# Three of four weight sums moved behind the third addition of a result, in a kernel of local attention and two expert layers

## The chip, the cores and the metric

One core of a Trainium2 chip runs the whole program. The metric is the device time of one execution in microseconds (us). Before the change it is 838.9 us, the median of three runs (838.24 to 839.41).

## The reference

The computation has three stages on 2 x 768 tokens of 512 channels. The change is in the third, where each token's channels go through four experts, weighted by normalized probabilities:

```python
def _moe2_ref(x, domain_probs, w1, w2):
    p = domain_probs / (domain_probs.sum(-1, keepdims=True) + 1e-09)
    out = np.zeros((N, D), dtype=np.float32)       # N = 1536, D = 512, E = 4, F = 1024
    for e in range(E):
        h = np.maximum(x @ w1[e], 0.0)
        out += p[:, e:e + 1] * (h @ w2[e])
    return out
```

Ahead of it stand attention (a window of 16 positions and block summaries) and a layer of 512 to 2048 to 512 channels with a PReLU.

## The kernel before

Every matrix operand is split in two parts of reduced precision, a high one (a copy on ScalarE) and a remainder (a subtraction on GpSimd or VectorE), and a product is three matmuls.

The third stage runs in 32 units `s`: 16 quarters of an expert (256 of the 4 x 1024 hidden channels) for each of two halves of the tokens; `NQ` = `UA` = 16. In a unit `e_steps` makes the first-layer products by a scheme of seven multiplications of quarter matrices (`p1` to `p7`), which needs sums of weight quarters (`e_sums`) besides the quarters. In the first half of the tokens (and in the last two units) `l2b` multiplies the hidden values by the second-layer weights, in six results of 128 tokens: six matmuls accumulate in a PSUM tile of pool `ps_2` (three buffers), and one VectorE instruction multiplies by the probability and adds to `acc2` (line 824; line 822 in the first unit of a half). In units 16 to 29, of the second half, the second layer uses a scheme of seven multiplications too, and that needs four sums of second-layer weights from two neighbouring units. They are made in advance, in the first half, and stored to DRAM (`dt`): `t_sums` makes them on VectorE, in place in the raw weight tiles `rb` (line 437), and `t_split` makes high part (ScalarE, line 441) and remainder (GpSimd, line 442) of each and stores both (line 416). Seven units do so, those with odd `s` from 1 to 13, each 28 / 7 = 4 subtractions of 128x512.

The order of the work. `standard(s, ...)` runs a unit: the products of the first layer, with the last two of the unit before it among them (`p1`, `p4` of the unit before, `p2`, `p6`, `p3` of the unit before, `p5`, `p7`), and then the six results `l2b` of the unit before, among which `merge` spreads the steps of `e_prep(s + 1)`: the loads, splits and sums for the next unit. In the seven units these are 14 steps: `t_sums`, the split of A11 and A12, `e_sums`, the splits of S1 and S2, of S3 and S4 and of A22, a load, two splits of second-layer weights, a load, and the four `t_split`. A split is one copy on ScalarE (line 386), one remainder on GpSimd (line 387) and stores.

TensorE and ScalarE execute in the order of the code (`tc.manual_schedule` with these two engines). The order on VectorE, GpSimd and the queue of SyncE that issues the DMAs is set by a planner when the program is built: it takes, by its own estimates, an instruction whose operands are ready, and of several ready ones the one that stands earlier in the code. `tc.issue_after(ins)` puts what is traced in its block behind `ins` on the queue of `ins`'s engine; `mark[s, 1, 1]` is the VectorE instruction that ends the result of `p7` of unit `s` (line 690).

ScalarE copies the PSUM tile `cb` of `p1` (line 678, tile `p`) before `p6` accumulates further into `cb` (line 655).

Of the kernel before, what the change touches and what calls it, by code (L numbers as in the profile page):

```python
# [12 lines left out]
ALU = mybir.AluOpType  # L13
# [79 lines left out]
def kernel(  # L93
# [15 lines left out]
    nc = tc.nc  # L109
# [22 lines left out]
    acc2 = acc.rearrange("p (t e) -> p t e", t=NT)  # L132
# [234 lines left out]
    def e_load_a(s):  # L367
        q = s % NQ
        t = wp.tile([P, 4, 2 * P], F32, tag="raw", name="ra", bufs=3)
        nc.sync.dma_start(out=t[:, 1:3].rearrange("p a c -> p (a c)"), in_=wb_in[0, 2 * q])  # L370
        nc.sync.dma_start(out=t[:, 0:4:3], in_=wb_in[0, 2 * q + 1].rearrange("p (a c) -> p a c", a=2))
        pw["a", s] = t

    def e_load_b(s):
        q = s % NQ
        if s % 2:
            t = gp.tile([P, 2, DM], F32, tag="rb", name="rb", bufs=1)
        else:
            t = wp.tile([P, 2, DM], F32, tag="raw", name="rb", bufs=3)
        nc.sync.dma_start(out=t, in_=wb_in[1, 2 * q:2 * q + 2].rearrange("i p n -> p i n"))  # L380
        pw["b", s] = t

    def e_split(pool, k, src, n=DM):
        hi = pool.tile([P, n], F32R, tag="h", name=f"w{k}h")
        lo = pool.tile([P, n], F32R, tag="l", name=f"w{k}l")
        nc.scalar.activation(hi, src, AF.Copy)  # L386
        nc.gpsimd.tensor_tensor(lo, src, hi.bitcast(F32), op=ALU.subtract)  # L387
        return hi, lo

    def e_sums(s):  # L390
        r = pw["a", s]
        s12 = wp.tile([P, 2, 2 * P], F32, tag="e", name="s12")
        s34 = wp.tile([P, 2, 2 * P], F32, tag="t", name="s34")

        def go(eng):
            eng.tensor_tensor(s12[:, 0], r[:, 0], r[:, 3], op=ALU.add)
            eng.tensor_tensor(s12[:, 1], s12[:, 0], r[:, 1], op=ALU.subtract)
            eng.tensor_tensor(s34[:, 0], r[:, 1], r[:, 0], op=ALU.subtract)
            eng.tensor_tensor(s34[:, 1], r[:, 2], s12[:, 1], op=ALU.subtract)

        if s % 2 == 0 and quad(s - 1 + NQ):
            with tc.issue_after(mark[s - 1, 0, 0]):
                go(nc.vector)
        else:
            go(nc.gpsimd)
        pw["s", s] = s12, s34

    def quad(s):
        return UA <= s < UB
# [4 lines left out]
    def put(dst, pair):  # L414
        for h, t in enumerate(pair):
            nc.sync.dma_start(out=dst[:, h], in_=t.bitcast(F32))
# [12 lines left out]
    def t_view(s, i):  # L429
        d = 2 * P * (i in (1, 2))  # L430
        return pw["b", s - i % 2][:, :, d:d + 2 * P]

    def t_sums(s):
        t1, t2, t3, t4 = (t_view(s, i) for i in range(4))
        with tc.issue_after(mark[s, 1, 1]):
            for y, p, q in ((t1, t3, t1), (t3, t2, t3), (t2, t2, t1), (t4, t4, t2)):
                nc.vector.tensor_tensor(y, p, q, op=ALU.subtract)

    def t_split(s, i):
        t, hi, lo = t_view(s, i), xh[t_place(i)], xl[t_place(i)]  # L440
        nc.scalar.activation(hi, t, AF.Copy)
        nc.gpsimd.tensor_tensor(lo, t, hi.bitcast(F32), op=ALU.subtract)
        put(dt[unit(s), i], (hi, lo))
# [16 lines left out]
    def named(s, names, hi, lo):  # L460
        for i, name in enumerate(names):
            ws[s, name] = hi[:, i * 2 * P:(i + 1) * 2 * P], lo[:, i * 2 * P:(i + 1) * 2 * P]

    def e_fetch(s):
        q = s % NQ
        for names in PARTS[1:3]:
            named(s, names, *get(wpool[0], lambda h: da[q, names[0]][:, h]))
        if not quad(s):
            for f in range(2):
                ws[s, f] = get(wpool[1], lambda h: dw[q, f][:, h])  # L470

    def e_load_again(s):
        if s >= 2 * NQ:
            return
        q = s % NQ
        if s == NQ:
            t = wp.tile([P, 3, 2 * P], F32, tag="raw", name="rc", bufs=3)
        else:
            t = gp.tile([P, 3, 2 * P], F32, tag="rb", name="rc", bufs=1)
        pw["a", s] = t  # L480
        nc.sync.dma_start(out=t[:, 0:2].rearrange("p a c -> p (a c)"), in_=wb_in[0, 2 * q])
        nc.sync.dma_start(out=t[:, 2], in_=wb_in[0, 2 * q + 1][:, 2 * P:])

    def e_prep(s):
        if s >= 2 * NQ:
            return []
        def part(names, src, pool=wpool[0]):
            pair = e_split(pool, 0, src, len(names) * 2 * P)
            named(s, names, *pair)
            if s < NQ and names in PARTS[1:3]:  # L490
                put(da[s, names[0]], pair)

        if s >= NQ:
            return [
                lambda: e_fetch(s),
                lambda: part(PARTS[0], pw["a", s][:, 0:2].rearrange("p a c -> p (a c)")),
                lambda: part(PARTS[3], pw["a", s][:, 2], wa22),
                lambda: e_load_again(s + 1),
            ]

        def second(i):
            ws[s, i] = e_split(wpool[1], 1, pw["b", s][:, i])
            n = 2 * P if s % 2 and quad(s + NQ) else DM
            put(dw[s, i][:, :, 0:n], [x[:, 0:n] for x in ws[s, i]])

        def flat(t):
            return t.rearrange("p a c -> p (a c)")

        steps = [
            lambda: part(("A11", "A12"), flat(pw["a", s][:, 1:3])),  # L510
            lambda: e_sums(s),
            lambda: part(("S1", "S2"), flat(pw["s", s][0])),
            lambda: part(("S3", "S4"), flat(pw["s", s][1])),
            lambda: part(("A22",), pw["a", s][:, 3], wa22),
        ]
        if s + 1 < NQ:
            steps.append(lambda: e_load_a(s + 1))
        for i in range(2):
            steps.append(lambda i=i: second(i))
        if s + 1 < NQ:  # L520
            steps.append(lambda: e_load_b(s + 1))
        else:
            steps.append(lambda: e_load_again(s + 1))
        if s % 2 == 0 and quad(s - 1 + NQ):
            steps.insert(0, lambda: t_sums(s - 1))
            steps += [lambda i=i: t_split(s - 1, i) for i in range(4)]
        return steps

# [4 lines left out]
    def split3(ps, terms):  # L533
        n = len(terms)
        for i, (a, c) in enumerate(terms):
            ins = nc.tensor.matmul(ps, a, c, start=(i == 0), stop=(i == n - 1))  # L536
        return ins
# [121 lines left out]
    bs, fs, mark = {}, {}, {}  # L659
# [150 lines left out]
    def l2b(s, i):  # L810
        b, q = divmod(s, NQ)
        t, half, e = b * NAC + i, i // (NAC // 2), q * NE // NQ
        tt = slice(i % (NAC // 2) * P, (i % (NAC // 2) + 1) * P)
        ps = ps_2.tile([P, DM], F32, tag="l2", name="l2")
        terms = []
        for f in range(2):
            (wh, wl), (gh, gl) = ws[s, f], gs[s, f, half]
            terms += [(gh[:, tt], wh), (gh[:, tt], wl), (gl[:, tt], wh)]
        split3(ps, terms)
        pe = prob_sb[:, t, e:e + 1]  # L820
        if q == 0:
            nc.vector.tensor_scalar(acc2[:, t], ps, pe, None, op0=ALU.mult)
        else:
            nc.vector.scalar_tensor_tensor(acc2[:, t], ps, pe, acc2[:, t], op0=ALU.mult, op1=ALU.add)  # L824
        if q == NQ - 1:
            nc.sync.dma_start(out=out[t * P:(t + 1) * P, :], in_=acc2[:, t])

# [7 lines left out]
    def l2_steps(u):  # L835
        n, c0, size = units[u]
        return [lambda d=d: l2a(n, d, c0, size) for d in range(KD)]
# [96 lines left out]
    with tc.manual_schedule(engines={mybir.EngineType.PE, mybir.EngineType.Activation}):  # L934
        left, keep = [], []
        l2 = l2_steps(len(units) - 1)[KD // 2:]
# [46 lines left out]
        for s in range(UA):  # L983
            l2, left, _ = standard(s, l2, left)
# [3 lines left out]
        for a in range(UA, UB, 2):  # L988
            q = l2_quad(a)
# [16 lines left out]
            old, done = q, k  # L1006
        paired(UB, "1..2..6...5..7...4...3...", old[done:], splits, 3)
        l2, left = [lambda i=i: l2b(UB, i) for i in range(NAC)], []
        for s in range(UB + 1, 2 * NQ):
            l2, left, keep = standard(s, l2, left)  # L1010
# [62 lines left out]
```

## Time and profile before

| | |
|---|---|
| median of the runs | 838.9 us (838.24 to 839.41) |
| the profiled execution, its own time | 837.95 us |
| its span, first to last instruction | 836.2 us |
| TensorE matmul busy | 814.4 us, 97% |
| TensorE weight load busy | 745.3 us, 89% |
| VectorE busy | 618.2 us, 74% |
| ScalarE busy | 427.4 us, 51% |
| GpSimd busy | 294.0 us, 35% |
| chain that ended last, TensorE's share | 92% |

Times in the trace are counted from the start of the span. PE is the matmuls of TensorE, PEld its weight loads, DVE is VectorE, ACT ScalarE, POOL GpSimd, SPq the queue of SyncE. The seven units with `t_sums` lie from 340 to 570 us, one in about 31.2 us, and repeat one another closely; the first of them is read below, where the additions are still line 822.

### The profile page before, as it was taken

The numbers are of one execution on the slowest core, as the hardware profiler recorded it, in microseconds if no ns is written. First come the engines' busy times: TensorE is split into PE (matmuls) and PEld (weight loads), VectorE is DVE, ScalarE is ACT, GpSimd is POOL, SyncE is SP. The second block draws the span as 40 slices with busy tenths as digits, with TensorE's granted clock in tenths as the row PEclk, the third lists the DMA queues.
The fourth block names the chain that finished last, engine by engine and source line by source line (L and its number), as shares of the span: only waits on it lengthen the run. The fifth ranks groups of instructions, "written<-read, shape, count | busy, mean of one in ns | idle before, by whom it ended". The sixth has DMA issues, their size and how long they took to land.

```text
span 836.2 us, 14453 instructions
## 1 busy us (share of the span) xinstructions
PE 814.4 (97%) x5000; PEld 745.3 (89%) x5000; DVE 618.2 (74%) x1315; ACT 427.4 (51%) x1050; POOL 294.0 (35%) x265
## 2 busy tenths in 40 slices
PE   3799999999999999999999999999999999999998
PEld 3699999888888888988988988988999999999997
DVE  6998667999994446587687687687667677768765
ACT  4999995543442323454454454455455454455430
POOL 0000000000013100376886886889243444354330
PEclk9799999999999999999999999999999999999999
DMA  9999412233222100266866867879776756767621
GB/s 321 283 299 298 156 46 102 101 100 102 84 92 74 53 1 0 101 223 229 304 234 231 290 215 252 289 240 321 241 228 203 256 197 229 238 217 231 200 74 75
DMA packets 97496, 155.37 MB, mean 186 GB/s; under 512 B 9872, under 2 KB 48272, under 8 KB 97424
## 3 DMA queue, kind: packets, MB, share of 16 engines
q1 hardware_dynamic: 96848, 154.18, 55.0%
q8 instruction: 39, 0.64, 0.3%
q14 instruction: 33, 0.27, 0.1%
q10 hardware_dynamic: 576, 0.28, 0.1%
HBM read 106.71 MB, written 47.71 MB: 185 GB/s over the span
## 4 chain that ended last, share of the span: by engine, by line
PE 92%; ACT 4%; DVE 2%; DMA 1%; issue 0%; ACTq 0%
PE l L536 48%; PE cb L655 16%; PE l2q L777 13%; PE cd L655 8%; PE ca L655 4%; PE s L215 1%; ACT sm L234 1%; ACT sm L253 1%; PE xps L277 1%; PE pt L259 1%; DMA alpha_sb<-in_alpha 1%; ACT ptb L152 1%; DMA kw<-in_kw 1%; DVE vs L179 0%; DVE sm L225 0%; DVE vcat L192 0%
## 5 line engine op out<-in xcount | busy, mean ns | idle before, releaser
L387 POOL TENSOR_TENSOR w0l<-ra,w0h 128x256 fp32r<-128x256 f32 (+1 forms) x32 | 36.8, 1151 | 357.4 <-ACT w0h L386 357.4
L824 DVE SCALAR_TENSOR_TENSOR acc<-l,prob_sb,acc 128x512 f32<-128x512 f32 x101 | 74.5, 745 | 24.7 <-PE l L536 24.6
L788 DVE SCALAR_TENSOR_TENSOR acc<-l2q,prob_sb,acc 128x256 f32<-128x256 f32 x156 | 71.2, 479 | 27.3 <-PE l2q L777 25.4
L536 PE MATMUL l<-xh,w0h 128*128 128x512 f32 (+1 forms) x240 | 84.6, 352 | 0.1
L536 PE MATMUL l<-gh,w1h 128*128 128x512 f32 (+1 forms) x240 | 83.4, 350 | 0.0
L536 PE MATMUL l<-xl,w0h 128*128 128x512 f32 (+1 forms) x240 | 83.3, 347 | 0.0
L536 PE MATMUL l<-xh,w0l 128*128 128x512 f32 (+1 forms) x240 | 83.2, 347 | 0.0
L536 PE MATMUL l<-gh,w1l 128*128 128x512 f32 (+1 forms) x240 | 83.0, 347 | 0.0
L536 PE MATMUL l<-gl,w1h 128*128 128x512 f32 (+1 forms) x240 | 81.5, 347 | 0.0
L536 PE MATMUL l<-w1h,gh 128*128 128x512 f32 x192 | 75.6, 394 | 0.0
L536 PE MATMUL l<-w1h,gl 128*128 128x512 f32 x192 | 75.2, 392 | 0.0
L536 PE MATMUL l<-w1l,gh 128*128 128x512 f32 x192 | 75.1, 391 | 0.0
L678 ACT ACTIVATE u<-cb 128x384 f32<-128x384 f32 x64 | 31.3, 489 | 51.7 <-PE cb L655 51.7
L561 DVE SCALAR_TENSOR_TENSOR l<-m,beta,l 128x512 f32<-128x512 f32 (+1 forms) x60 | 38.6, 646 | 23.8 <-ACT m L555 23.6
L555 ACT ACTIVATE m<-l 128x512 f32<-128x512 f32 (+1 forms) x60 | 30.6, 512 | 46.6 <-PE l L536 46.3
L536 PEld LDWEIGHTS l<-xh,w0h 128*128 128x128 f32 x240 | 45.5, 189 | 6.2 <-ACT ptb L152 0.3
L536 PEld LDWEIGHTS l<-gh,w1h 128*128 128x128 f32 x240 | 45.5, 189 | 5.7
L536 PEld LDWEIGHTS l<-gh,w1l 128*128 128x128 f32 x240 | 45.5, 189 | 5.6
L536 PEld LDWEIGHTS l<-xl,w0h 128*128 128x128 f32 x240 | 45.4, 189 | 5.5
L536 PEld LDWEIGHTS l<-gl,w1h 128*128 128x128 f32 x240 | 45.4, 189 | 5.5
L536 PEld LDWEIGHTS l<-xh,w0l 128*128 128x128 f32 x240 | 45.4, 189 | 5.6
L387 POOL TENSOR_TENSOR w0l<-s,w0h 128x512 fp32r<-128x512 f32 x32 | 47.8, 1513 | 2.9 <-ACT w0h L386 2.9
(165 smaller groups left out, 2527.7 us busy)
## 6 DMA issues: line engine op xcount, KB each, us to landing
raw<-in_wa SPq DMA_DIRECT2D x32, 512.0 KB, 3.8
rb<-in_wb SPq DMA_DIRECT2D x16, 512.0 KB, 4.5
ra<-in_wb SPq DMA_DIRECT2D x32, 256.0 KB, 3.6
dt<-xh SPq DMA_DIRECT2D x28, 256.0 KB, 3.4
dt<-xl SPq DMA_DIRECT2D x28, 256.0 KB, 4.3
bh<-dt SPq DMA_DIRECT2D x28, 256.0 KB, 3.7
bl<-dt SPq DMA_DIRECT2D x28, 256.0 KB, 3.6
q<-in_qh SPq DMA_DIRECT2D x24, 256.0 KB, 5.2
```

The costliest lines, as they stand in the source:

```text
L152: nc.scalar.activation(dst, src, AF.Copy)
L215: nc.tensor.matmul(sp[:, u], q[:, u // 2, u % 2], kw[:, :, u // 2, u % 2], start=True, stop=True)
L234: nc.scalar.activation(sm[:, u], sm[:, u], AF.Exp, bias=mx[:, u:u + 1], scale=-1.0, accum_out=sume[:, u:u + 1],)
L387: nc.gpsimd.tensor_tensor(lo, src, hi.bitcast(F32), op=ALU.subtract)
L536: ins = nc.tensor.matmul(ps, a, c, start=(i == 0), stop=(i == n - 1))
L555: nc.scalar.activation(m, gs[i, c0][0], AF.Relu, scale=-1.0)
L561: nc.vector.scalar_tensor_tensor(ps, m, beta[:, i:i + 1], ps, op0=ALU.mult, op1=ALU.add)
L655: nc.tensor.matmul(ps, l, r, start=(first and i == 0), stop=(i == len(terms) - 1), skip_group_check=True)
L678: nc.scalar.activation(v[name], ps, AF.Copy)
L777: nc.tensor.matmul(ps, l, r, start=(first and j == 0), stop=(j == len(terms) - 1), skip_group_check=True)
L788: nc.vector.scalar_tensor_tensor(dst, ps, pe, dst, op0=ALU.mult, op1=ALU.add)
L824: nc.vector.scalar_tensor_tensor(acc2[:, t], ps, pe, acc2[:, t], op0=ALU.mult, op1=ALU.add)
```

## The change

Of the four subtractions of `t_sums` the first stays where it was. The other three become a second step, which `e_prep` inserts behind the split of A22, and which `issue_after` puts behind the latest traced addition of a result. With 15 steps among six results that is the third addition.

```diff
-    def t_sums(s):
+    def t_sums(s, part):
         t1, t2, t3, t4 = (t_view(s, i) for i in range(4))
-        with tc.issue_after(mark[s, 1, 1]):
-            for y, p, q in ((t1, t3, t1), (t3, t2, t3), (t2, t2, t1), (t4, t4, t2)):
+        steps = ((t1, t3, t1), (t3, t2, t3), (t2, t2, t1), (t4, t4, t2))
+        with tc.issue_after(mark["l2"] if part else mark[s, 1, 1]):
+            for y, p, q in steps[part:3 * part + 1]:
                 nc.vector.tensor_tensor(y, p, q, op=ALU.subtract)
...
-            steps.insert(0, lambda: t_sums(s - 1))
+            steps.insert(0, lambda: t_sums(s - 1, 0))
+            steps.insert(6, lambda: t_sums(s - 1, 1))
             steps += [lambda i=i: t_split(s - 1, i) for i in range(4)]
...
-            nc.vector.tensor_scalar(acc2[:, t], ps, pe, None, op0=ALU.mult)
+            added = nc.vector.tensor_scalar(acc2[:, t], ps, pe, None, op0=ALU.mult)
         else:
-            nc.vector.scalar_tensor_tensor(acc2[:, t], ps, pe, acc2[:, t], op0=ALU.mult, op1=ALU.add)
+            added = nc.vector.scalar_tensor_tensor(acc2[:, t], ps, pe, acc2[:, t], op0=ALU.mult, op1=ALU.add)
+        mark["l2"] = added.ins
```

## Rows read from the trace of the kernel before

**Rows 1.** Windows, six products with, without subtractions: stretch, length, busy time (instructions) by engine.

```profile
core 0: us, PE busy (x) PEld busy (x) DVE busy (x) ACT busy (x) POOL busy (x), PEclk, DMA share, GB/s
357.12:365.53 8.41, 8.41 (x37) 6.69 (x37) 7.49 (x10) 4.92 (x10) 5.91 (x4) 1.00 0.53 196
372.85:381.05 8.20, 8.20 (x38) 6.76 (x37) 5.14 (x7) 4.15 (x8) 8.12 (x9) 1.00 1.03 339
```

**Rows 2.** Timeline of weight loads at product 6: start, duration, engine, line, operation, [idle before].

```profile
363.51 0.19 PEld L536 LDWEIGHTS l<-w1h,gl 128*128 128x128 f32 x1
364.04 0.19 PEld L536 LDWEIGHTS l<-w1h,gh 128*128 128x128 f32 x1 [0.34 <-DVE acc L822]
```

**Rows 3.** Timeline of VectorE: subtractions (437), additions 2, 3 (822).

```profile
359.84 1.78 DVE L437 TENSOR_TENSOR rb<-rb 128x512 f32<-128x512 f32 x1
361.55 0.74 DVE L822 TENSOR_SCALAR acc<-l,prob_sb 128x512 f32<-128x512 f32 x1
362.21 1.12 DVE L437 TENSOR_TENSOR rb<-rb 128x512 f32<-128x512 f32 x1
363.25 0.74 DVE L822 TENSOR_SCALAR acc<-l,prob_sb 128x512 f32<-128x512 f32 x1
363.91 1.11 DVE L437 TENSOR_TENSOR rb<-rb 128x512 f32<-128x512 f32 x1
...
365.61 1.81 DVE L437 TENSOR_TENSOR rb<-rb 128x512 f32<-128x512 f32 x1
```

**Rows 4.** Groups of instructions of VectorE, whole span: xcount | busy us, mean ns | idle before.

```profile
L437 DVE TENSOR_TENSOR rb<-rb 128x512 f32<-128x512 f32 x28 | 40.9, 1460 | 0.0
...
L344 DVE TENSOR_TENSOR t<-t,e 128x512 f32<-128x512 f32 x32 | 21.9, 686 | 0.1
```

**Rows 5.** Timeline of ScalarE: last copy of the weight sums, copy of p1.

```profile
367.45 0.63 ACT L441 ACTIVATE xh<-rb 128x512 fp32r<-128x512 f32 x1 [1.25 <-DVE rb L437]
367.99 0.47 ACT L678 ACTIVATE p<-cb 128x384 f32<-128x384 f32 x1
```

**Rows 6.** Timeline of weight loads: the first one of p6.

```profile
368.52 0.19 PEld L655 LDWEIGHTS cb<-xeh,w0h 128*128 128x128 f32 x1
```

**Rows 7.** Timeline of GpSimd: remainders (387) beside the subtractions.

```profile
359.62 1.46 POOL L387 TENSOR_TENSOR w0l<-ra,w0h 128x512 fp32r<-128x512 f32 x1 [5.79 <-ACT w0h L386]
361.03 1.75 POOL L387 TENSOR_TENSOR w0l<-s,w0h 128x512 fp32r<-128x512 f32 x1
362.74 1.74 POOL L387 TENSOR_TENSOR w0l<-s,w0h 128x512 fp32r<-128x512 f32 x1
364.44 1.19 POOL L387 TENSOR_TENSOR w0l<-ra,w0h 128x256 fp32r<-128x256 f32 x1
365.59 1.28 POOL L387 TENSOR_TENSOR w1l<-rb,w1h 128x512 fp32r<-128x512 f32 x1
```

**Rows 8.** Timelines of VectorE and GpSimd in a later unit.

```profile
641.64 0.55 DVE L741 TENSOR_TENSOR fr<-fr,fe 128x384 f32<-128x384 f32 x1
642.11 1.37 DVE L735 TENSOR_TENSOR ft<-fr,ft 128x384 f32<-128x384 f32 x1
...
641.89 1.17 POOL L746 TENSOR_TENSOR xl<-ft,xh 128x384 fp32r<-128x384 f32 x1 [7.26 <-ACT xh L745]
```

**Rows 9.** Timeline of VectorE in the same unit: a sum, its dependent, line 729 between.

```profile
639.70 0.55 DVE L739 TENSOR_TENSOR fr<-fe,fr 128x384 f32<-128x384 f32 x1
640.30 0.57 DVE L729 TENSOR_TENSOR cd<-cd,u 128x384 f32<-128x384 f32 x1
640.78 0.55 DVE L740 TENSOR_TENSOR fe<-ft,fe 128x384 f32<-128x384 f32 x1
```

**Rows 10.** First-layer weights: issue, landing (page: KB, us), first reader on GpSimd.

```profile
366.19 1.12 SPq L370 DMA_DIRECT2D ra<-in_wb  x1
...
ra<-in_wb SPq DMA_DIRECT2D x32, 256.0 KB, 3.6
...
373.51 0.77 POOL L396 TENSOR_TENSOR s<-ra 128x256 f32<-128x256 f32 x1
```

## The prediction

> **What bounds the kernel now.** I read first where TensorE itself is held up in the stretch of the change, then what releases it, then the three queues around it (VectorE, GpSimd, ScalarE) in order of time. Names: additions 1 to 6 are those of the six results of a unit (line 824, or 822 in the first such unit), products 1 to 6 TensorE's work for them, subtractions 1 to 4 the sums of second-layer weights (line 437), remainders GpSimd's instructions on line 387.
>
> TensorE is in work all the time here: in the stretch with the six products it is busy 8.41 of 8.41 us [rows 1]. But the same six products take 8.20 us in a unit without subtractions, so 0.21 us are lost in one with them. The lost time is at product 6: its weight load comes 0.34 us late, released by an addition [rows 2], and the row shows which: addition 3 ends at 363.25 + 0.74 = 363.99 and the load starts at 364.04 [rows 2, 3]. Product 6 needs the accumulator that addition 3 empties (three buffers), and addition 3 is late because subtractions 1 and 2 stand ahead of it. There are seven such units (28 subtractions, [rows 4]), so 7 x 0.21 = 1.5 us is all that shorter waiting there can give.
>
> The Trainium skill, "Perfetto Trace Analysis", Identifying the Most-Contended Engine, says that the busy share of matmuls is a bad measure of what is left and that of weight loads a good one. By the matmul row (8.41 of 8.41) the sum would start from nothing to gain; by the weight loads' own wait it would start from 7 x 0.34 = 2.4 us. The two windows show 0.21, between the two, and that is what the sum uses.
>
> **A second wait, just as tight.** ScalarE works in the order of the code: the four copies of the new weights (line 441), then the copy of product p1 of the next unit (line 678). The last copy starts at 367.45, when subtraction 4 has ended at 365.61 + 1.81 = 367.42; p1's copy runs from 367.99 to 368.46 [rows 3, 5]. Product p6 writes into the accumulator which that copy reads, and its weight load starts at 368.52, 0.06 us after it [rows 6]; in all seven units the distance is 0.05 to 0.06 us, as between addition 3 and product 6 (0.05), so TensorE waits there too, by a hair. So the end of subtraction 4 decides: later, and TensorE loses as much at p6; not earlier, and the 0.21 us saved at product 6 are lost again at p6.
>
> **When subtractions end.** They take 1.11 to 1.81 us although a VectorE operation of the same size with both operands in SBUF takes 0.69 us while GpSimd is idle [rows 3, 4]. Each ends 0.55 us after the end of a GpSimd remainder: 361.08 + 0.55 = 361.63, 362.78 + 0.55 = 363.33, 364.48 + 0.55 = 365.03, 366.87 + 0.55 = 367.42 [rows 3, 7]. The remainder that follows is stretched in turn: 1.75 and 1.74 us where an unhindered one takes 1.28; counted from the end of the subtraction a long one takes 1.15 us, the short one of A22 0.61 [rows 7]. So they take turns, whoever is under way is let finish. Subtraction 4 started 0.02 us after a remainder (365.61 against 365.59) and had to wait for all of it. Two VectorE operations in a row don't get through together either: one at 641.64, a GpSimd operation asks at 641.89 while it runs, the next VectorE one, from 642.11, ends only at 643.48, 0.42 after GpSimd's end [rows 8].
>
> The Trainium skill, "SBUF — State Buffer", Who interferes with whom, states a lock of this kind: a VectorE instruction with two SBUF inputs and a GpSimd instruction that reads SBUF block each other, by order of issue. Priced without it, each subtraction at its mean of 1.46 us [rows 4], the sum below would come to +0.99 us a unit and 6.9 in all instead of 8.3; the rows above bear the lock out, and the sum goes by them.
>
> **The change part by part.** Nothing is added or removed: four subtractions, six additions, four copies, the same stores. Subtraction 1 stays. (1) Subtraction 2 leaves its place ahead of addition 3. That addition then follows addition 2 at 362.21 and ends at 362.95 (its product, three before product 6, was done around 361), so product 6, whose load is due at 363.74, doesn't wait: -0.21 a unit. (2) Subtraction 2 follows at 362.87. In the trace GpSimd starts its third remainder at 362.74, so the subtraction has lost the turn: the remainder ends at 362.74 + 1.28 = 364.02, the subtraction at 364.57, the short remainder of A22 at 365.18. (3) What comes next on VectorE is the planner's choice, and it decides the case.
>
> Order A: addition 4, then subtraction 3. The addition starts at 364.49, subtraction 3 0.66 later at 365.15, and the next long remainder 0.04 before the end of the last one, at 365.14. That is subtraction 4's geometry of today (an addition ahead of it, the short remainder running), lost by 0.02 us in all seven units; so it is lost again. Subtraction 3 ends at 365.14 + 1.28 + 0.55 = 366.97, the next remainder at 368.12, subtraction 4 at 368.67 instead of 367.42: 1.25 later. An addition between subtractions 3 and 4 doesn't alter this.
>
> Order B: subtraction 3 straight after subtraction 2. It waits for the short remainder, ends at 365.18 + 0.55 = 365.73; the next remainder ends at 366.88 and subtraction 4, issued in time even with one addition before it, at 367.43. That is today's 367.42, to the hundredth.
>
> Which order? The planner takes what it reckons ready, and a subtraction is ready only when the one before it is done (each overwrites what that one reads). By unhindered times VectorE has caught up by then, and addition 3 starts when product 3 is done. From its start subtraction 2 ends 0.66 + 0.69 = 1.35 us later by unhindered times; product 4 ends one product later than product 3, 8.20 / 6 = 1.37 us [rows 1, 3, 4]. By itself a tie. Today's order tells which way it falls: an addition stands ahead of every further subtraction. And where line 739 has a dependent (line 740), the planner put line 729 between them, though in the trace it became ready only 0.05 us after 739's end (640.25, started 640.30), in six units alike [rows 9]: it reckons TensorE's results a little earlier than they come, measured by VectorE. So I take order A, not by much.
>
> (4) ScalarE in order A: the last copy and p1's copy start 1.25 later, p6's load too, at 369.77 instead of 368.52. After product 6's late load (0.30 beyond the due time, 0.21 lost) TensorE caught up 0.09; with as much here a unit loses 1.16, with none 1.25. The 0.21 of (1) are within this, since p6 then waits for ScalarE alone. Sum: 7 x 1.16 to 1.25 = 8.1 to 8.8, taken as 8.3 (order B: 7 x 0 to -0.03). (5) Stores: the subtractions issue none, but the copies' stores on the SP queue wait for them, and the load of the next first-layer weights stands behind one. It is issued at 366.19, lands some 3.6 us later, and is first read at 373.51 [rows 10]; in order A it moves by about 2 us, to land near 372, still in time: it costs nothing, and without that cover GpSimd's next sums would come later by what is missing. (6) Additions 4 to 6 come later by up to 1.3 us in A; the next products that need their accumulators start at 372.85: nothing.
>
> The profiled execution took 837.95 us (span 836.2), the median of the runs is 838.9; stage and sum are differences, so I add them to the median: 838.9 + 8.3 = 847.2.
>
> **Rivals.** *Not slower, order B* (chance 0.35): subtraction 3 follows subtraction 2 directly. For it: the tie above. Against: today's alternation. The wait moves from product 6 to p6, the time stays: 838.7 (838.0 to 839.4). It decides from the moment that product 4 counts as later than subtraction 2's end.
> *Faster* (0.04): subtraction 2 gets its turn ahead of the third remainder, subtraction 4 ends a remainder earlier, and p6 waits for nothing: -1.5 us, 837.4. Against: it is issued at 362.87, 0.13 us too late. By the weight loads' wait it would be 2.4 us (836.5).
> *All three behind the sixth addition* (0.04): subtraction 2 issued at about 366.2 and, by the same turns, subtraction 4 done near 370.2 (an estimate), 2.8 us a unit, 858. It would need the planner to put work that is not ready ahead of work that is. That the change does nothing is excluded: the order after addition 3 is enforced.
> *Order A* has 0.57, counting that the turn at 365.14 is lost.
>
> **How the numbers follow.** A measurement of this kernel can tell 0.2% (1.7 us) from no change. Slower: 0.57 + 0.04 = 0.61. Same: order B, and most of the faster case, whose 1.5 us is below the bound: 0.36. Faster: 0.03. Order A alone spans 846.5 to 848.2; with B at 0.35 the range has to reach it: 838.0 to 848.2, leaving out the two small cases and edges.
>
> **What would show it.** Right: no late load at product 6; p6's load some 1.2 us late, released by ScalarE, once a unit, seven times; subtraction 3 ending near 367.0 and 4 near 368.7 where they ended at 365.0 and 367.4; an addition between subtractions 2 and 3. Wrong: subtractions 2 and 3 adjacent and subtraction 4 where it was (order B), or p6's load on time while product 6 is not late (faster). A loss elsewhere than at p6 would mean that another queue was reordered.

## The result

The changed kernel takes 847.95 us (median of 4 runs, 846.01 to 848.29), the kernel before 838.61 us beside it (838.24 to 839.41): a ratio of 1.0111, 95% interval 1.0099 to 1.0124. It is slower by 9.3 us; forecast were 847.2 us and a loss of 8.3, by order A.

### The profile after

The profiled execution took 847.68 us, its span 845.9. The first view answers to [rows 1]: the windows of the first of the seven units, the six products and then the products p1 to p7 that follow. Below it the same second window of the kernel before.

```profile
core 0: us, PE busy (x) PEld busy (x) DVE busy (x) ACT busy (x) POOL busy (x), PEclk, DMA share, GB/s
357.82:366.02 8.20, 8.20 (x37) 6.76 (x37) 7.29 (x10) 4.46 (x9) 5.70 (x5) 1.00 0.55 201
366.02:374.78 8.76, 7.60 (x43) 7.28 (x42) 6.66 (x9) 3.92 (x8) 8.76 (x7) 1.00 0.87 296
```

```profile
365.53:372.85 7.32, 7.32 (x44) 7.32 (x43) 5.83 (x9) 3.44 (x8) 7.32 (x7) 1.00 0.84 289
```

The six products take 8.20 us and no longer 8.41: the wait at product 6 is gone. The stretch behind them takes 8.76 instead of 7.32. So this unit gains 0.21 and loses 1.44, net 1.23. The starts of subtraction 1 in the first and the seventh unit (359.84 and 547.36 before, 360.55 and 555.33 after) give the mean: units 31.25 us apart before and 32.46 after, 1.21 more, 8.5 us in seven. The two spans differ by 9.7 us (836.2 and 845.9); the other 1.2 are 0.7 ahead of the first unit, where the two kernels do the same work, and 0.5 behind the seventh (below, in the part on the prediction).

Who holds TensorE up, by the waits of its weight loads from 340 us on (total, times, longest):

```profile
PEld cb L657 <- ACT p L680: 10.4, 7, 1.5
PEld cb L657 <- ACT u L680: 0.5, 1, 0.5
```

In the kernel before:

```profile
PEld l L536 <- DVE acc L824: 2.1, 6, 0.4
PEld l L536 <- DVE acc L822: 0.3, 1, 0.3
```

Seven waits for the copy of p1, once a unit, where there were seven for an addition. ScalarE and the load of p6 in the first unit (timelines; [rows 5, 6] before):

```profile
367.72 1.16 ACT L442 ACTIVATE xh<-rb 128x512 fp32r<-128x512 f32 x2 [4.56 <-DVE rb L438]
369.43 0.63 ACT L442 ACTIVATE xh<-rb 128x512 fp32r<-128x512 f32 x1 [0.55 <-DVE rb L438]
369.97 0.47 ACT L680 ACTIVATE p<-cb 128x384 f32<-128x384 f32 x1
...
370.49 0.19 PEld L657 LDWEIGHTS cb<-xeh,w0h 128*128 128x128 f32 x1 [1.48 <-ACT p L680]
```

The chain is subtraction 4, the last copy, p1's copy (until 370.44), the load 0.05 later. VectorE, subtractions (now line 438) and additions, and GpSimd's remainders beside it ([rows 3, 7] before):

```profile
360.55 1.78 DVE L438 TENSOR_TENSOR rb<-rb 128x512 f32<-128x512 f32 x1
362.25 1.40 DVE L824 TENSOR_SCALAR acc<-l,prob_sb 128x512 f32<-128x512 f32 x2
363.57 1.72 DVE L438 TENSOR_TENSOR rb<-rb 128x512 f32<-128x512 f32 x1
365.22 0.74 DVE L824 TENSOR_SCALAR acc<-l,prob_sb 128x512 f32<-128x512 f32 x1
365.88 1.81 DVE L438 TENSOR_TENSOR rb<-rb 128x512 f32<-128x512 f32 x1
367.61 0.74 DVE L824 TENSOR_SCALAR acc<-l,prob_sb 128x512 f32<-128x512 f32 x1
368.27 1.12 DVE L438 TENSOR_TENSOR rb<-rb 128x512 f32<-128x512 f32 x1
...
363.46 1.29 POOL L387 TENSOR_TENSOR w0l<-s,w0h 128x512 fp32r<-128x512 f32 x1
364.71 1.18 POOL L387 TENSOR_TENSOR w0l<-ra,w0h 128x256 fp32r<-128x256 f32 x1
365.85 1.28 POOL L387 TENSOR_TENSOR w1l<-rb,w1h 128x512 fp32r<-128x512 f32 x1
367.10 1.74 POOL L387 TENSOR_TENSOR w1l<-rb,w1h 128x512 fp32r<-128x512 f32 x1
```

Additions 2 and 3 stand together (x2), addition 4 between subtractions 2 and 3, as in order A. Subtraction 2 is issued at 363.57, 0.11 after a long remainder (363.46), and ends 0.55 after that one's end, 364.75. Subtraction 3 starts at 365.88, 0.03 after the next long remainder (365.85), waits for all of it and ends at 367.14 + 0.55 = 367.69; subtraction 4 ends at 369.39. The table counts the ends from the start of subtraction 1, in the first unit, so that the execution's own shift (0.7 us here) drops out; the mean distance from unit to unit, taken as above, is free of it too and of all that stands ahead of the seven units. The other kernels in it are the experiments below.

| kernel | subtraction 3 ends | subtraction 4 ends | units apart | time, its kernel before beside it |
|---|---|---|---|---|
| before [rows 3] | 5.18 | 7.58 | 31.25 | 838.61 |
| after | 7.14 | 8.84 | 32.46 | 847.95, 838.61 |
| subtractions 2 and 3 adjacent | 5.88 | 7.59 | 31.20 | 837.92, 838.27 |
| A22's remainder last | 6.44 | 8.14 | 31.76 | 842.13, 838.27 |
| copies behind p1's copy | 7.14 | 8.84 | 31.01 | 836.68, 838.27 |
| the same copies, without the change | 5.18 | 7.59 (6.45 in the six other units) | 31.23 | 838.35, 838.27 |
| behind the fourth addition | 7.13 | 8.84 | 32.46 | 848.01, 837.97 |
| one column written by GpSimd | 6.00 | 7.70 | 31.33 | 838.22, 838.30 |

### The profile page after: what moved, and what is told of

Its sections match the earlier page's. It is cut to its first block, busy times and chain, and to the rows that moved or that the text cites. A ratio compares the mean times of both kernels' runs of the same rounds, so it can differ in the third digit from the quotient of the medians.

```text
span 845.9 us, 14459 instructions
## 1 busy us (share of the span) xinstructions
PE 815.6 (96%) x5000; PEld 745.5 (88%) x5000; DVE 620.8 (73%) x1315; ACT 426.6 (50%) x1050; POOL 294.0 (35%) x265
## 4 chain that ended last, share of the span: by engine, by line
PE 81%; DVE 11%; DMA 6%; ACT 2%; issue 1%; SPq 0%; ACTq 0%
PE l L538 40%; PE cb L657 14%; PE l2q L779 12%; PE cd L657 8%; DVE rb L438 5%; PE ca L657 3%; DVE acc L826 3%; DMA q<-in_qh 2%; PE s L215 2%; PE xps L277 1%; DMA acc<-in_vt 1%; DMA vcat<-in_vw 1%; PE pt L259 1%; DMA raw<-in_wa 1%; DVE gl L692 1%
## 5 line engine op out<-in xcount | busy, mean ns | idle before, releaser
L657 PE MATMUL cb<-xeh,w0h 128*128 128x384 f32 x128 | 43.7, 341 | 8.1 <-ACT p L680 8.1
```

Of the source, the lines that this page charges most:

```text
L657: nc.tensor.matmul(ps, l, r, start=(first and i == 0), stop=(i == len(terms) - 1), skip_group_check=True)
```

## The experiments

The theory: the place of one addition makes subtraction 3 lose its turn with GpSimd, subtraction 4 ends a long remainder later, and ScalarE's order passes that on to p6. The rivals are that a later start as such makes the subtractions late, that the two engines slow each other by the amount of their work, and that something else than ScalarE's order carries the loss.

### Subtractions 2 and 3 adjacent

In the changed kernel, addition 4 is queued behind subtraction 3 (`third` holds it while the fourth result is traced; the block left out is the addition, lines 824 and 826).

```diff
-            for y, p, q in steps[part:3 * part + 1]:
-                nc.vector.tensor_tensor(y, p, q, op=ALU.subtract)
+            for k, (y, p, q) in enumerate(steps[part:3 * part + 1]):
+                done = nc.vector.tensor_tensor(y, p, q, op=ALU.subtract)
+                if part and k == 1:
+                    mark["third"] = done.ins
...
+        third = mark.pop("third", None)
+        with tc.issue_after(third) if third is not None else ExitStack():
...
```

> The changed kernel with addition 4 put behind subtraction 3, so that subtractions 2 and 3 stand next to each other (order B of the prediction); nothing else differs. Theory (the turns with GpSimd, by the place of one addition): subtraction 3 waits for the short remainder only, subtraction 4 ends where it ended before the change, and p6 waits as little as there: 838.6 us, between 838.0 and 839.4. Rival (starting three subtractions after addition 3 is in itself too late, whatever stands between them): they end late again, 846 to 848 us.

Measured: 837.92 us against 838.27, ratio 0.9995 (0.9983 to 1.0006). The timeline of VectorE (subtractions 2 and 3 merged as x2) with GpSimd's short and next long remainder, and then the waits of the weight loads:

```profile
363.23 2.86 DVE L438 TENSOR_TENSOR rb<-rb 128x512 f32<-128x512 f32 x2
366.02 0.74 DVE L828 TENSOR_SCALAR acc<-l,prob_sb 128x512 f32<-128x512 f32 x1
366.68 1.12 DVE L438 TENSOR_TENSOR rb<-rb 128x512 f32<-128x512 f32 x1
...
364.36 1.19 POOL L387 TENSOR_TENSOR w0l<-ra,w0h 128x256 fp32r<-128x256 f32 x1
365.51 1.74 POOL L387 TENSOR_TENSOR w1l<-rb,w1h 128x512 fp32r<-128x512 f32 x1
```

```profile
PEld cb L659 <- ACT p L682: 1.5, 7, 0.2
```

Subtraction 3 ends at 366.09, 0.55 after the short remainder (365.55). The three moved subtractions start after addition 3 as in the changed kernel, and the whole loss is gone: the place of one addition makes it. What is saved at product 6 is for the most part lost again at p6, as order B said: the weight loads stand idle there 0.21 us a unit (1.5 / 7), and the units lie 31.20 us apart, 0.05 less than before the change and 0.19 more than without either wait (31.01, below).

### The short remainder last

In the changed kernel, the split of A22, with the load step next to it, stands behind the two splits of second-layer weights; the later subtractions stay behind the third addition.

```diff
+            a22, load = steps[4:6]
+            steps[4:6] = []
+            steps[6:6] = [a22, load]
             steps.insert(0, lambda: t_sums(s - 1, 0))
-            steps.insert(6, lambda: t_sums(s - 1, 1))
+            steps.insert(5, lambda: t_sums(s - 1, 1))
```

> The changed kernel with the split of A22 moved behind the two splits of second-layer weights, so that GpSimd makes its short remainder (0.74 us) after two long ones and not before them; VectorE's order and all work stay the same. Theory (a subtraction loses its turn when GpSimd starts its next remainder 0.02 us ahead of it): while subtraction 3 is held back by addition 4, a long remainder is still running, so subtraction 3 keeps its turn and ends 0.70 us earlier, subtraction 4 too; p6's load is 0.7 us less late in each of the seven units: 843.0 us (842.3 to 844). Rival (the two engines only slow each other by the amount of their work, which is the same): 848 us within 0.7.

Measured: 842.13 us against 838.27, ratio 1.0059 (1.0040 to 1.0078). VectorE's order is the changed kernel's, GpSimd's work is the same; the timeline of addition 4, subtraction 3 and the long remainder beside it, and the waits of the weight loads:

```profile
369.00 0.74 DVE L827 TENSOR_SCALAR acc<-l,prob_sb 128x512 f32<-128x512 f32 x1
369.66 1.11 DVE L438 TENSOR_TENSOR rb<-rb 128x512 f32<-128x512 f32 x1
...
368.48 1.74 POOL L387 TENSOR_TENSOR w1l<-rb,w1h 128x512 fp32r<-128x512 f32 x1
```

```profile
PEld cb L660 <- ACT p L683: 5.4, 7, 0.8
```

Subtraction 3, held back by addition 4, finds a long remainder still running and gets its turn at that one's end (370.22 + 0.55 = 370.77). It and subtraction 4 end 0.70 us earlier than in the changed kernel, as forecast; the waits fall from 10.4 to 5.4 us. The time is a little below the range given (842.3 to 844). The amount of work would have given 848.

### Copies behind p1's copy, with the change and without

ScalarE's last three copies of weight sums, with their remainders and stores, are taken from the end of `e_prep` into the next unit, behind the copies after p1 and p4. The same edit is made in the changed kernel and in the kernel before.

```diff
...
-            for f in [p1] + left[:1] + [p2, p6] + left[1:] + [p5, p7]:
+            for f in [p1] + left[:1] + held + [p2, p6] + left[1:] + [p5, p7]:
                 f()
             side = e_prep(s + 1)
+            held[:] = side[-3:] if s % 2 and quad(s + NQ) else []
+            side = side[:len(side) - len(held)] + [lambda: None for _ in held]
```

> The changed kernel with ScalarE's copies of the second, third and fourth weight sum (and their remainders and stores) put behind the copy of p1 and the copy after p4 of the next unit; the subtractions stay as late as the change makes them. Theory (the whole loss passes through ScalarE's order, subtraction 4 to its copy to p1's copy to p6): p6 waits for nothing, product 6 neither: 838.6 - 1.5 = 837.1 us (836.6 to 838.0). Rival (late subtractions also hold up something else, VectorE's additions or GpSimd's next sums): between 839 and 848 us, with another late load.

> The kernel before with the same three copies put behind the copy of p1; the subtractions stay where they were. Theory: product 6 still waits for addition 3, 0.21 us in each of seven units, and p6's wait was only a hair: 838.5 us (838.0 to 839.0). Rival (p6's wait was the larger one already): 837.1 us, as with the change.

Measured: with the change 836.68 us against 838.27, ratio 0.9985 (0.9974 to 0.9996); without it 838.35, ratio 0.9999 (0.9990 to 1.0008). The timeline of ScalarE with the change, first unit, and the waits of the weight loads without the change:

```profile
367.42 0.49 ACT L680 ACTIVATE p<-cb 128x384 f32<-128x384 f32 x1 [4.13 <-PE cb L657]
368.45 0.49 ACT L691 ACTIVATE gh<-cb 128x384 fp32r<-128x384 f32 x1 [0.55 <-PE cb L657]
368.85 1.66 ACT L442 ACTIVATE xh<-rb 128x512 fp32r<-128x512 f32 x3
```

```profile
PEld l L536 <- DVE acc L824: 2.3, 7, 0.4
PEld l L536 <- DVE acc L822: 0.3, 1, 0.3
```

With the change, subtraction 4 ends as late as ever (8.84 after the start of subtraction 1), but p1's copy no longer stands behind it, and from 340 to 570 us no wait of a matmul or a weight load is left. The whole loss went through ScalarE's order; late subtractions hold up nothing else. Without the change, the waits of product 6 stay, and so does the time. The copies alone gain nothing and the change alone loses; together they free both waits, and the kernel is 1.6 us faster than before, as far as the interval reaches (0.04 to 0.26%); the distance of the units says 7 x 0.24 = 1.7.

The kernel with the copies alone shows something more. Up to subtraction 4 its work on VectorE and GpSimd stands in the order of the kernel before, and GpSimd is recorded 0.02 us ahead of subtraction 4 as there. Yet subtraction 4, which lost this turn in all seven units of the kernel before, wins it in six of seven here. In the second unit:

```profile
396.83 0.68 DVE L437 TENSOR_TENSOR rb<-rb 128x512 f32<-128x512 f32 x1
...
396.81 1.86 POOL L387 TENSOR_TENSOR w1l<-rb,w1h 128x512 fp32r<-128x512 f32 x1
```

With the copies late nothing waits for subtraction 4, so the time doesn't show it.

### Behind the fourth addition

```diff
-            steps.insert(6, lambda: t_sums(s - 1, 1))
+            steps.insert(7, lambda: t_sums(s - 1, 1))
```

> The changed kernel with subtractions 2 to 4 put behind the fourth addition and not the third; the order on VectorE is then additions 2, 3 and 4, subtraction 2, addition 5, subtraction 3, addition 6, subtraction 4. Theory (turns): subtraction 2 is issued 0.66 us later, still inside the third remainder, and ends where it ended; subtractions 3 and 4 lose and keep the same turns as in the changed kernel: no change against it, 847.9 us (846.5 to 848.8). Rival (each addition ahead of a subtraction delays the end by its own 0.66 us): 847.9 + 7 x 0.66 = 852.5 us.

Measured: 848.01 us against 837.97, ratio 1.0129 (1.0094 to 1.0165). The interval alone nearly reaches the rival's 1.017; the trace decides, with units 32.46 us apart as in the changed kernel. Subtraction 2 follows three additions:

```profile
360.86 2.06 DVE L824 TENSOR_SCALAR acc<-l,prob_sb 128x512 f32<-128x512 f32 x3
362.84 1.06 DVE L438 TENSOR_TENSOR rb<-rb 128x512 f32<-128x512 f32 x1
...
362.05 1.30 POOL L387 TENSOR_TENSOR w0l<-s,w0h 128x512 fp32r<-128x512 f32 x1
```

Issued 0.66 us later, it lasts 1.06 instead of 1.72 and ends at the same point, 0.55 after the same remainder; subtraction 4 ends at 8.84 as in the changed kernel. A later start costs nothing as long as it meets the same turn.

### The changed kernel again

> The changed kernel once more, unaltered, beside the kernel before. Its profiled execution showed one wait more than the theory has, 0.5 us ahead of one product in a unit of the second half, and 9.3 us in all instead of 8.3. If that wait belongs to the change, it stands in this profile too and the difference is 9.3 again; if it came by chance, the profile shows only the seven waits at p6 and the difference is 8.3 to 8.8.

Measured: 846.11 us against 837.97, ratio 1.0091 (1.0074 to 1.0108): a loss of 8.1. Neither expectation fits as it stands. The 0.5 us wait of the first profile is missing, but one of the seven at p6 is nearly so too: of 9.3 us of waits at p6, that one has 0.34 and each of the others 1.49.

```profile
PEld cb L657 <- ACT p L680: 9.3, 7, 1.5
```

The timeline, subtraction 3 and the long remainder it meets, in its first unit and then in its seventh:

```profile
365.78 1.81 DVE L438 TENSOR_TENSOR rb<-rb 128x512 f32<-128x512 f32 x1
...
365.76 1.29 POOL L387 TENSOR_TENSOR w1l<-rb,w1h 128x512 fp32r<-128x512 f32 x1
...
560.57 0.68 DVE L438 TENSOR_TENSOR rb<-rb 128x512 f32<-128x512 f32 x1
...
560.54 1.86 POOL L387 TENSOR_TENSOR w1l<-rb,w1h 128x512 fp32r<-128x512 f32 x1
```

In the seventh unit subtraction 3 got the turn: 0.68 us, and GpSimd's remainder is the one that waited. The turn is close enough to fall either way, and each one won saves about 1.15 us (1.49 - 0.34). Whether it spreads the runs of the changed kernel (844.1 to 848.3 in both series) is not shown: 29 runs of the kernel before are spread as widely, from 836.2 to 841.0.

### One column written by GpSimd

If 0.025 us decide, a very short instruction in GpSimd's queue has to turn all seven.

```diff
+        def step():
+            with tc.issue_after(mark["low"]):
+                mark["step"] = nc.gpsimd.memset(nudge, 0.0).ins
...
+            a22 = steps[4]
+            steps[4] = lambda: (a22(), step())
```

`mark["low"]` is the last remainder, `nudge` a tile of 128x1; the next long remainder is queued behind `mark["step"]`.

> The changed kernel with one instruction more on GpSimd in each of the seven units, a write of one column (128x1) between the short remainder of A22 and the long one behind it. VectorE's order stays that of the changed kernel, addition 4 between subtractions 2 and 3. Theory (subtraction 3 loses its turn by some 0.025 us): the write makes GpSimd start its long remainder later than VectorE its subtraction 3, which then ends right after the short remainder, near 365.8 in the clock of the first unit; subtraction 4 ends near 367.4 as before the change, and the time falls back to 838.6 us (838.0 to 839.5) although work was added. Rival (the added distance from the front, not the turn, makes subtraction 3 late): 846 to 848.5 us.

Measured: 838.22 us against 838.30, ratio 0.9995 (0.9980 to 1.0010). The timeline of VectorE from addition 4 on, and of GpSimd beside it:

```profile
366.33 0.74 DVE L834 TENSOR_SCALAR acc<-l,prob_sb 128x512 f32<-128x512 f32 x1
366.99 0.68 DVE L440 TENSOR_TENSOR rb<-rb 128x512 f32<-128x512 f32 x1
...
366.95 0.10 POOL L506 MEMSET nudge<- 128x1 f32 x1
367.00 1.82 POOL L388 TENSOR_TENSOR w1l<-rb,w1h 128x512 fp32r<-128x512 f32 x1
```

The write of 0.10 us, with the remainder queued behind it, puts the long remainder at 367.00, 0.01 behind subtraction 3 (366.99), which now takes 0.68 us; so in all seven units. The waits of the weight loads:

```profile
PEld cb L667 <- ACT p L690: 2.4, 7, 0.3
```

VectorE's order is that of the changed kernel, addition 4 in between, GpSimd has more to do, and the loss is gone but for what the time can't tell: the units lie 31.33 us apart, 0.08 more than before the change where the changed kernel has 1.21. The turn is the cause.

## Why the prediction was right

*What bounds the kernel*: both waits stand as read. Product 6's is gone in the changed kernel (8.20 for 8.41), and freeing p1's copy alone (838.35) or product 6 alone (837.92) gives nothing that can be told, both together 1.6 us, where 1.5 were counted.

*The turns*: subtractions 2, 3 and 4 were put at 364.57, 366.97 and 368.67 in the clock of the kernel before. They end 4.74, 7.14 and 8.84 after the start of subtraction 1, at 364.58, 366.98 and 368.68 in that clock. Priced at the mean of 1.46 us the loss would have been 6.9 us; the loss of 8.5 in the seven units goes with the lock, and so do the experiments on order. But part of it was luck. The prediction put the remainder 0.01 us ahead of subtraction 3 (365.14 and 365.15) and took the turn for lost because subtraction 4 had lost one like it seven times. Such a turn went the other way once in the repeated run, and six times of seven in the kernel before with late copies; each one won would have taken about 1.15 us off the loss.

*The order on VectorE* was the uncertain step, a tie read from the planner's habits. Order A came, and the adjacent pair shows that order B was worth what the rival said (837.92; 838.7 forecast). Whether the planner chose A for the reason given, no run shows. The range, 838.0 to 848.2, held both orders, so the time alone says little, and 847.95 lies near its upper end; it is the ends of the subtractions and the waits at p6 that bear the account out.

*The sum* was slightly short. A unit lost 1.21 us on average, within the 1.16 to 1.25 worked out, which makes 8.5 in seven units where 8.3 was taken. What no step foresaw is the wait of 0.5 us in a unit of the second half, for another copy of ScalarE. It is in the profiles of the changed kernel and of the one with the fourth addition, where TensorE lost the full 1.2 us in the seventh unit, and in none of the others. Its path can be read. GpSimd's work behind the seventh unit isn't put off with TensorE's: a remainder there that came at 577.02 comes at 585.06, 8.0 later, the VectorE instruction that came at 578.16 (line 690; 692 after) at 587.31, 9.2 later. So that instruction meets another one of GpSimd's (line 632, started 0.02 us ahead of it). It takes 1.42 us instead of 0.57, VectorE is late by some 0.6 us from there on, ScalarE's copy `u` stands behind its results and ends at 599.86, and the weight load starts 0.05 later; first the kernel before, then the changed one:

```profile
578.16 0.57 DVE L690 SCALAR_TENSOR_TENSOR gl<-c,gh 128x384 fp32r<-128x384 f32 x1
...
587.31 1.42 DVE L692 SCALAR_TENSOR_TENSOR gl<-c,gh 128x384 fp32r<-128x384 f32 x1
...
599.37 0.49 ACT L680 ACTIVATE u<-cb 128x384 f32<-128x384 f32 x1
...
599.91 0.19 PEld L657 LDWEIGHTS cb<-xeh,wfh 128*128 128x128 f32 x1 [0.54 <-ACT u L680]
```

The median of the time rose by 9.3 us, 8.3 to 10.4 by its interval; the 8.5 and 0.5 of the trace, 9.0 together, lie within it.

*The stores* (step 5) went another way without cost: the planner put the loads of first-layer weights ahead of the store that waits for subtraction 3, and they are not delayed at all (issued at 365.91, in a clock that is 0.7 us on, where it was 366.19).

*The rivals*: the turn ahead of the third remainder did not occur, and behind the sixth addition was not tried; behind the fourth nothing was added, so its 858 us, worked out with turns, are not refuted but lack a run.

## What to carry to other kernels

When two engines block each other, as VectorE and GpSimd do here, an instruction does not end a fixed time after its start but after the other engine's instruction that it meets; list those ends, and see which one a moved instruction will meet. Before moving work off one wait, look for the second wait that is satisfied only just in time (here 0.05 us after the copy of p1): it takes the gain, and a delay goes through it nearly in full (1.25 us late, 1.21 lost). Where a turn hangs on a few hundredths of a microsecond, a reordering on either engine, or a tiny instruction, decides more than the amount of work, and a forecast that counts on the turn carries a chance.

## What the runs showed of the hardware

One write of 128x1 on GpSimd, 0.09 to 0.10 us long, in each of seven units took the units from 32.46 to 31.33 us apart, 7.9 us in a run, since it turned seven losses. The write itself was under way when subtraction 3 started (366.95 and 366.99) and didn't hold it up (0.68 us).

By the starts in the records GpSimd was ahead of the losing subtraction by 0.02 to 0.03 us in the fourteen turns of the kernels before and after. At the same recorded distance the subtraction also won: six times at 0.02 in the kernel before with late copies, once at 0.03 in the repeated run, where the kernel with the fourth addition lost one at 0.03. So at that distance the recorded starts don't say who wins. The Trainium skill, "SBUF — State Buffer", Who interferes with whom, says of the ports that VectorE and GpSimd share that they are an exclusive lock and that the order of issue decides who blocks. The durations here agree with a lock (0.68 or 1.81 us for the same subtraction, 1.28 or 1.86 for the remainder); on the order of issue the recorded starts can't speak at 0.02 to 0.03 us.

The additions, which read one operand from PSUM, took 0.73 to 0.75 us beside a busy GpSimd throughout, where the subtractions, with both in SBUF, took 0.68 to 1.82.
